# Decode attention over a 256 MiB cache: eight heads per unit, 8 MB loads into shared slots, P spread by masks, O picked on VectorE

## The chip, the cores and the metric

One core of a Trainium2 chip. The metric is the device time of one execution in microseconds (us). The core has TensorE (PE), VectorE (DVE), ScalarE (ACT), GpSimd (POOL), a SyncE queue (SP) that issues most loads, and sixteen DMA engines behind it. Ratios: the mean time of one kernel's fast runs over that of the kernel before in the same rounds, with a 95% interval, so not quite the ratio of the medians that are quoted beside them. Where I turn a ratio into us, I multiply by 670.5. The rounds of the experiments ran on three different chips (K15, K2, tail and all three edits on one, the three runs on rows and the one with two extra transposes on another, the rest on a third), so runs are compared through these ratios.

## The reference, cut to what matters

```python
xn = layernorm(x)                        # x: 4 x 1 x 640, bf16
q = (xn @ wq).reshape(B, Sq, H, Dh)      # B 4, H 32, Dh 128
scores = einsum('bhqd,bhkd->bhqk', q, k_cache) * Dh ** -0.5    # k_cache: 4 x 32 x 4096 x 128
p = softmax(scores)
o = einsum('bhqk,bhkd->bhqd', p, v_cache)
out = x + o.reshape(B, Sq, H * Dh) @ wo + gated_mlp(xn)
```

K and V are 134 MB each, every byte is used once, and there is one query per head. The weights add 14 MB.

## The kernel before

A unit is four heads of one batch entry: 4 MB of K or V, as 128 partitions with one row of 32 KB each. A group is the four units (batch entries) of the same heads. Units rotate through five whole tiles, and the tile framework inserts the waits.

```python
HG = 4; M = P // HG; T = Sk // M          # T = 128 tokens in a partition's row
kvpool = ctx.enter_context(tc.tile_pool(name="kvpool", bufs=5))      # 5 x 32 KB per partition

def load_unit(cache, key, u, cuts=(0, T)):
    g, b = divmod(u, B)
    t_sb = kv_tile(f"{key}{u}")
    src = cache[b, g * HG:(g + 1) * HG].rearrange("e (m t) d -> (e m) (t d)", t=T)
    for t0, t1 in zip(cuts[:-1], cuts[1:]):
        nc.sync.dma_start(out=t_sb[:, t0 * Dh:t1 * Dh], in_=src[:, t0 * Dh:t1 * Dh])

def emit_T(u, ch):                        # VectorE: 128x2048 f32 transpose in 32x32 blocks
    nc.vector.transpose(kT[:], kw[:, ch * n:(ch + 1) * n])
# ... (cut) emit_S: eight PE matmuls of 128x512 for each such block give the scores S in PSUM

def z_fill(g, bb):                        # ScalarE spreads the transposed P out of PSUM into Zb
    # ... (cut)
    nc.scalar.copy(out=dst, in_=src[:, 2 * bb + b1])

def emit_O(g, bb):                        # O of two units goes to SBUF, f32 matmuls select from it
    nc.scalar.copy(out=O_sb[:], in_=O_ps[:])

# the last V unit alone, token by token, so that O comes out with d on the partitions:
for t in range(T):
    nc.tensor.matmul(ol_ps[:], lhsT=vv[:, t, :], rhs=zc, start=(t == 0), stop=(t == T - 1))
nc.vector.tensor_tensor(out=oL[:, :, 3:4], in0=ol_ps[:, :, None], in1=..., op=ALU.mult)
emit_proj(g, oL, last=True)               # eight matmuls with wo
```

## Time and profile before

| | before |
|---|---|
| time | 670.65 us median of 3 (670.45 to 670.73) |
| span of the profiled execution | 668.2 us |
| bytes by DMA | 282.65 MB in 12,035 packets |
| DMA, busy | 98.7% of the span in one queue |
| DVE, PE, ACT busy | 48%, 50%, 9% |

How to read it: work on an engine that is half idle costs nothing unless something waits for it.

### The profile page before, as it was taken

To read this page: it belongs to the slowest core of one execution; us is meant where nothing else is said; L and a number is where in the kernel's file an instruction comes from. 1 tells how busy PE (TensorE), PEld (TensorE's weight loads), DVE (VectorE), ACT (ScalarE), POOL (GpSimd) and SP (SyncE) were. 2 spreads that over 40 slices of the span, in tenths; PEclk is the share of its full clock that TensorE was granted. 3 is DMA by queue.
4 is the path that set the end of the run, shared out by engine and by line. 5 is a ranking of instruction groups with operands and counts; after the bars stand their busy time and mean duration, and the time that the engine had idled before them with its cause. 6 is when DMAs were issued, how large, how long until landed. Compare 5 with 4: busy or idle time off the path is not lost.

```text
span 668.2 us, 6403 instructions
## 1 busy us (share of the span) xinstructions
PE 333.3 (50%) x2781; PEld 140.6 (21%) x2781; DVE 318.8 (48%) x252; ACT 60.4 (9%) x184; POOL 10.6 (2%) x43
## 2 busy tenths in 40 slices
PE   0646563456543654337455364345743365443645
PEld 0511121122111321113121031111311122111323
DVE  5179863365543455542555534346543345543300
ACT  1100210012000200003000030001200021000300
POOL 1100000000000000000000000000000000000000
PEclk9997577878777787666866677876777778567776
DMA  8999999999999999999999999999999999999996
GB/s 329 429 420 429 437 437 421 429 441 420 431 437 421 436 434 433 422 434 434 423 434 434 427 433 432 429 430 435 429 432 431 430 431 433 428 434 429 430 425 243
DMA packets 12035, 282.65 MB, mean 423 GB/s; under 512 B 1396, under 2 KB 2024, under 8 KB 3304
## 3 DMA queue, kind: packets, MB, share of 16 engines
q1 hardware_dynamic: 11928, 282.25, 98.7%
q8 instruction: 21, 0.34, 0.2%
q14 instruction: 6, 0.05, 0.0%
q0 software_dynamic: 64, 0.00, 0.0%
q10 hardware_dynamic: 16, 0.01, 0.0%
HBM read 282.25 MB, written 0.01 MB: 422 GB/s over the span
## 4 chain that ended last, share of the span: by engine, by line
DMA 66%; PE 12%; issue 11%; DVE 9%; ACT 2%; SPq 0%; DVEq 0%; ACTq 0%
DMA k<-in_A_k_cache_dram 52%; DMA v<-in_A_v_cache_dram 7%; DVE kT L323 6%; PE O L427 5%; DMA wo_last<-in_A_wo_dram 5%; PE S L341 3%; DMA wq<-in_A_wq_dram 2%; ACT p L369 2%; PE x L382 1%; PE misc L444 1%; PE misc L207 1%; DVE m L348 1%; PE misc L352 0%; DVE om L447 0%; ACT O_sb L435 0%
## 5 line engine op out<-in xcount | busy, mean ns | idle before, releaser
L323 DVE STREAM_TRANSPOSE kT<-k 128x2048 f32<-128x2048 f32 x128 | 284.6, 2280 | 216.7 <-DMA k<-in_A_k_cache_dram 214.3
L341 PE MATMUL S<-kT,QZ 128*32 128x512 bf16 x1024 | 200.8, 532 | 261.3 <-DVE kT L323 258.9
L341 PEld LDWEIGHTS <-QZ 128*32 128x32 bf16 x1024 | 57.0, 114 | 400.8 <-issue 390.0
L427 PE MATMUL O<-v,Zb 128*32 128x512 bf16 x992 | 91.1, 463 | 8.9 <-DMA v<-in_A_v_cache_dram 8.9
L427 PEld LDWEIGHTS <-Zb 128*32 128x32 bf16 x992 | 42.1, 111 | 38.8 <-issue 24.1
L369 ACT ACTIVATE p<-S,negmax 128x1024 bf16<-128x1024 f32 x16 | 17.7, 1110 | 271.9 <-DVE negmax L363 271.9
L435 ACT COPY O_sb<-O 128x512 f32<-128x512 f32 x16 | 9.4, 586 | 239.7 <-PE O L427 239.7
L393 ACT COPY Zb<-x 32x128 bf16<-32x128 bf16 x128 | 27.3, 254 | 10.2 <-PE x L382 9.5
L382 PE MATMUL x<-IdP,p 128*128 128x128 bf16 x128 | 16.1, 305 | 18.9 <-ACT p L369 18.6
L447 DVE SCALAR_TENSOR_TENSOR om<-misc,rinv,MkH 16x512 bf16<-16x512 f32 x7 | 5.2, 739 | 38.3 <-PE misc L444 38.3
L444 PE MATMUL misc<-O_sb,SelG 128*16 128x128 f32 x112 | 16.9, 289 | 2.0 <-DVE rinv L403 1.5
L382 PEld LDWEIGHTS <-p 128*128 128x128 bf16 x128 | 12.0, 138 | 22.7 <-ACT p L369 22.7
L280 POOL COPY QZ<-q 32x16 bf16<-32x16 bf16 x32 | 7.9, 248 | 443.7 <-PE S L341 430.6
L444 PEld LDWEIGHTS misc<-O_sb,SelG 128*16 128x16 f32 x112 | 10.2, 100 | 8.1 <-ACT O_sb L435 2.4
L479 DVE TENSOR_TENSOR oL<-misc,rinv 128x8 bf16<-128x8 f32 (+1 forms) x2 | 0.3, 168 | 22.6 <-PE misc L477 22.6
L348 DVE TENSOR_REDUCE m<-S 128x1 f32<-128x512 f32 x8 | 5.5, 692 | 10.9 <-PE S L341 10.9
L373 DVE TENSOR_TENSOR rowsum<-rs 128x1 f32<-128x1 f32 x8 | 1.2, 154 | 17.0 <-ACT p L369 17.0
L352 PE MATMUL misc<-dg,ones_f 128*128 128x128 f32 x16 | 4.2, 346 | 9.0 <-DVE dg L350 9.0
L207 PE MATMUL misc<-xnT,wq 128*128 128x4 bf16 x160 | 4.6, 166 | 7.7 <-DMA wq<-in_A_wq_dram 7.7
L207 PEld LDWEIGHTS <-wq 128*128 128x128 bf16 x160 | 4.4, 104 | 7.9 <-DMA wq<-in_A_wq_dram 7.9
L210 DVE CAST q_bf<-misc 128x128 bf16<-128x128 f32 x1 | 0.3, 292 | 12.0 <-PE misc L207 12.0
L465 PE MATMUL proj<-wo,oT 128*4 128x320 bf16 x56 | 5.0, 298 | 1.9 <-DVE oT L458 1.9
(95 smaller groups left out, 76.4 us busy)
## 6 DMA issues: line engine op xcount, KB each, us to landing
k<-in_A_k_cache_dram SPq DMA_DIRECT2D x32, 4096.0 KB, 43.0
v<-in_A_v_cache_dram SPq DMA_DIRECT2D x31, 4096.0 KB, 41.1
wo<-in_A_wo_dram SPq DMA_DIRECT2D x7, 640.0 KB, 45.8
wq<-in_A_wq_dram SPq DMA_DIRECT2D x1, 3072.0 KB, 12.2
w_gmlp<-in_B_w_in_dram SPq DMA_DIRECT2D x1, 2160.0 KB, 21.4
wq<-in_A_wq_dram SPq DMA_DIRECT2D x1, 2048.0 KB, 16.7
v<-in_A_v_cache_dram SPq DMA_DIRECT2D x1, 2048.0 KB
v<-in_A_v_cache_dram SPq DMA_DIRECT2D x1, 1024.0 KB, 38.4
```

The source lines that it names most:

```text
L207: nc.tensor.matmul(q_ps[:, h, :], lhsT=wq_t[c][:, h * Dh:(h + 1) * Dh], rhs=xnT[:, c, :], start=(c == 0), stop=(c == DC - 1))
L280: nc.gpsimd.tensor_copy(out=qz[r0:r0 + 32, :, :, 8 + 8 * hd], in_=q3[r0:r0 + 32, :, c0:c0 + B].rearrange("p a b -> p b a"))
L323: nc.vector.transpose(kT[:], kw[:, ch * n:(ch + 1) * n])
L341: nc.tensor.matmul(S_ps[32 * q:32 * q + 32, :, :], lhsT=qz[:, b, kw, w0:w0 + 32], rhs=kT[:, i, :, kw // 2, :, kw % 2], start=(b == 0 and c ...
L348: nc.vector.tensor_reduce(out=m1[:], in_=S_ps[:].rearrange("p k m -> p (k m)"), axis=AX.X, op=ALU.max)
L369: nc.scalar.activation(out=p_i[:], in_=S_ps[:, 8 * i:8 * i + 8, None, :].to_broadcast((P, 8, HG, M)), func=ACT.Exp, bias=negmax[:, 0:1], s ...
L382: nc.tensor.transpose(x[:, t, :], p_bf[t // 8][:, t % 8].rearrange("p h m -> p (h m)"), IdP[:])
L393: nc.scalar.copy(out=dst, in_=src[:, 2 * bb + b1])
L427: nc.tensor.matmul(O_ps[32 * q:32 * q + 32, :, :], lhsT=Zb[bb][:, w0:w0 + 32], rhs=vv[:, e // 16, e % 16, :, :], start=(b1 == 0 and e < 4) ...
L435: nc.scalar.copy(out=O_sb[:], in_=O_ps[:])
L444: nc.tensor.matmul(oh[:], lhsT=SelG[:, bb, c].rearrange("p h b -> p (h b)"), rhs=O_sb[:, c, :], start=(bb == 0 and c == 0), stop=(bb == 1 ...
L447: nc.vector.scalar_tensor_tensor(out=om[:], in0=oh[:, None, :].to_broadcast((G, HG, Dh)), scalar=state.pop(("rinv", g))[:, 0:1], in1=MkH[: ...
```

## The change

The intent: double the row and the load (64 KB and 8 MB), halve the number of groups (eight to four), and make wo's rows 10 KB. A unit no longer fits the old tile, so K, V and wo share one array of five 4 MB slots, placed by hand. The new shapes also change how P reaches the V matmuls and how O leaves them.

```diff
-    HG = 4
+    HG = 8
...
-    kvpool = ctx.enter_context(tc.tile_pool(name="kvpool", bufs=5))
+    SL = T * Dh // 2
+    kv = const.tile([P, 5 * SL], BF16)
...
+    place = {("k", 0): 3, ("k", 1): 0, ("k", 2): 2, ("k", 3): 0}
+    for u in range(B, NU):
+        place[("k", u)] = 1 if u % 2 == 0 else 0
+    for u in range(NU):
+        place[("v", u)] = 3
+    place[("v", NU - 3)] = 1
+    place[("v", NU - 1)] = 0
+    first = {2: 1}
+    cuts = {("k", 0): (0, T // 2, T), ("k", 1): (0, T // 2, T), ("v", NU - 1): (0, 128, 192, 224, 240, T)}
+    for g in range(NG):
+        u = B * g + B - 1
+        if u < NU - 1:
+            cuts[("k", u)] = (0, T // 2, T)
+            first[u] = 0
...  P: a dense copy xd of the transposed P, then one masked spread for each head
+                nc.vector.tensor_copy(out=xd[r0:r0 + 32, :, 16 * half:16 * half + 16],
+                                      in_=x[r0:r0 + 32, :, r0:r0 + 32].rearrange("p t r -> p r t"))
...
-                nc.scalar.copy(out=dst, in_=src[:, 2 * bb + b1])
+                    nc.scalar.activation(out=dst, in_=src, func=ACT.Copy, scale=MkE[r0:r0 + 32, e:e + 1])
...  O: four masked picks in place of a copy and f32 selections
-        nc.scalar.copy(out=O_sb[:], in_=O_ps[:])
+        nc.vector.tensor_scalar(out=R, in0=O_ps[:, 0, :], scalar1=Mk4[:, 0:1], scalar2=None, op0=ALU.mult)
+        for c in range(1, 4):
+            nc.vector.scalar_tensor_tensor(out=R, in0=O_ps[:, c, :], scalar=Mk4[:, c:c + 1], in1=R, op0=ALU.mult, op1=ALU.add)
...  the order of work: the next load is put out ahead of the work on the current one
+    for i, item in enumerate(seq):         # K0 K1 K2 K3 V0 K4 V1 K5 V2 ... K15 V12 V13 V14 V15
+        if i + 1 < len(seq):
+            load_unit(seq[i + 1])
...  wo: eight heads at once into slot 2, the last group's in pieces of 4, 2, 1 and 1 heads
-            for h0, h1 in ((0, 2), (2, 3), (3, 4)):
+            for h0, h1 in ((0, 4), (4, 6), (6, 7), (7, 8)):
```

The token-by-token treatment of the last V unit is dropped: V15 goes the common way, with picks and one selection.

## The prediction

> **What bounds the kernel now.** I read the page's first two parts, then the queue table and the list of issues, then busy time by stretches, then the chain at the end, and last the waits of the load queue.
>
> ```profile
> PE 333.3 (50%) x2781; PEld 140.6 (21%) x2781; DVE 318.8 (48%) x252; ACT 60.4 (9%) x184; POOL 10.6 (2%) x43
> ...
> DMA  8999999999999999999999999999999999999996
> ...
> DMA packets 12035, 282.65 MB, mean 423 GB/s; under 512 B 1396, under 2 KB 2024, under 8 KB 3304
> ...
> q1 hardware_dynamic: 11928, 282.25, 98.7%
> ```
>
> No compute engine passes 50%; the DMA engines are full in every slice but the first and the last, and one queue holds them 98.7% of the span. So only three things can move the time: bytes (unchanged), the pace at which full engines move them, and the stretches in which they are not full. The stretches show the last two:
>
> ```profile
> 0.00:20.00 20.00, 2.69 (x86) 2.53 (x87) 8.96 (x36) 2.86 (x3) 2.71 (x11) 1.00 0.85 345
> 40.00:80.00 40.00, 25.81 (x126) 6.97 (x121) 34.38 (x21) 0.51 (x1) 0.98 (x4) 0.73 1.01 432
> 160.00:320.00 160.00, 78.67 (x606) 31.31 (x602) 76.11 (x51) 13.60 (x44) 1.97 (x8) 0.74 1.00 430
> 480.00:600.00 120.00, 58.28 (x440) 21.96 (x440) 58.20 (x35) 7.38 (x23) 0.00 (x0) 0.73 1.00 431
> 660.00:668.20 8.20, 3.47 (x72) 2.42 (x72) 0.65 (x2) 0.00 (x0) 0.00 (x0) 0.50 0.24 87
> ```
>
> The last two numbers are the DMA share and GB/s. From 40 to 600 us the share is 1.00 at 430 to 432 GB/s. In the first 40 to 80 us DVE is busy 34.4 of 40 us, so there DVE is nearly as tight as DMA; later it is under half. At the end:
>
> ```profile
> 633.62 30.23 DMA wo_last<-in_A_wo_dram
> 663.85 0.04 issue
> 663.89 1.30 PE proj L465 x8
> ```
>
> After the last byte of wo only eight projection matmuls, a cast and the store remain, about 4.3 us to the span's end at 668.2. The queue's waits tell how far loads run ahead:
>
> ```profile
> SPq L294 <- DVE kT L323: 302.6, 32, 15.3
> ...
> k<-in_A_k_cache_dram SPq DMA_DIRECT2D x32, 4096.0 KB, 43.0
> v<-in_A_v_cache_dram SPq DMA_DIRECT2D x31, 4096.0 KB, 41.1
> ```
>
> The queue waits for buffers to come free most of the time, but a 4 MB load takes 9.7 us (4.19 MB at 432 GB/s) and lands 43 us after issue: more than three others are queued ahead of it. Waiting for a buffer costs nothing now.
>
> **What the Trainium skill says.** "DMA: Bandwidth & Descriptors", section "Where 436 GB/s comes from", puts the ceiling of a core's sixteen engines at 435.2 GB/s. The trace agrees: 430 to 432 over long stretches. The same page, "Why small descriptors are slow (HBM only)", gives a fixed cost per packet and per descriptor, so longer rows should help; at 32 KB rows little of it can be left, since 431 is already 99% of 435. "Perfetto Trace Analysis", section "Optimization Strategy", says that the same gap repeating on the engine that should be saturated can mean too little room for the next tile. Before has no such gap; after is the kernel in which to look for it. "VectorE: DVE Perf Modes", section "Why PSUM operands drop a tier", holds an f32 operand in PSUM to the 1x rate; the reduce of 128x512 f32 from PSUM at 692 ns agrees (1.35 ns an element with its fixed cost), so I cost the new DVE reads of PSUM at that.
>
> **Part by part.**
>
> *Loads.* K and V go from 64 loads of 4 MB with 32 KB rows to 32 units of 8 MB with 64 KB rows (some cut in halves); wo rows go from 5 to 10 KB. The first nine 4-us windows add to 13.71 MB by 36 us; the stretch after 650 us holds 4.64 MB. So 264.3 MB took 614 us, 430.4 GB/s. At 435.2 it would take 607.3 us: 6.7 us is all that rows and load count could ever return. I take half of it to hang on each load or packet, and halve that: **-1.7 us**. wo alone is under 2% of the bytes.
>
> *Buffers.* Five whole tiles of 4 MB become five slots of 4 MB, two to a unit, so one unit is being used, one loads, and half a unit is spare. Nearly all V units share slots 3 and 4; K alternates between slots 0-1 and 1-2 and frees slot 1 first. The load after next is therefore issued only when the current V is used up, or when half the current K is transposed. A bubble appears if that is later than the end of the transfer in flight. Two lags are needed. Landing: 8.55 MB of weights and 4.19 MB of K0 had been moved at 33.8 us (sum of windows), DVE started on it at 36.6: 2.7 us. Issue to first bytes: first issue 0.74 us, no byte before 1.5 us: about 1.2 us (estimate). An 8 MB load takes 19.4 us.
> Steady state: K needs 4 transposes x 2.28 = 9.1 us to free slot 1, while V loads for 19.4 us; slack 19.4 - 9.1 - 2.7 - 1.2 = 6.4 us. V needs 64 matmuls, 4 to 7.2 us at the 2.0 to 3.6 us per 32 that the timeline shows; slack at least 8 us. No bubble.
> First group: K0 lands in halves at 36.6 and 46.3, K1 at 55.9 and 65.6, K2 whole at 85.0, K3 at 94.7 and 104.4, V0 at 123.8. DVE is done with K1 at 74.6, idles to 85, then needs sixteen transposes in a row: 36 us, to 121. K4 needs K3's second half, so it is issued at 121.1 and flows at 122.3; V0's bytes ended at 121.1. **+1.2 us.** Then V1 waits until V0 is used: S done 122.9; maximum, broadcast and negation 3.6 (reduce of 1024 about 1.2); table load 1.3; seven of eight exponentials 4.8; two rounds of transposes, 32-partition copies (0.65 each) and mask spreads to about 139; last 32 matmuls to 142. K4's bytes end at 141.7. **About +1.5 us.**
> Later groups: K's halves land 9.7 us apart and 1.31 MB of wo (3.0 us) is queued before V, and exp's table is in place; slack about 8 us. The last group's K is not halved: V14 is issued some 37.4 us after K15 lands, V13's bytes end at 39.1. **+0.3 us** on average.
>
> *Engines.* The 1024 K transposes' matmuls, 128 DVE transposes of 128x2048 and 128 P transposes stay. DVE gains 64 picks of O (128x128 from PSUM, 0.29 each like the 128x128 mask multiply: 19 us) and 32 copies of the dense transpose (0.65: 21 us): 319 becomes about 360 us, 54%. ACT loses sixteen O copies (9.4) and gains about 24 us of mask spreads and 4 us of exponentials: about 79 us. PE loses most of the 112 f32 selection matmuls (17 us). None sets the end; all lie beside loads.
>
> *Tail.* wo_last doubles to 1.31 MB, all behind V15. V15 lands about 3 us earlier relative to wo's end; its last four matmuls, four picks (1.2), one selection (0.5) and a multiply fit in that. Fourteen of sixteen projection matmuls run before wo's last piece, against none of eight now. **-1.0 us.** The small x load leaves the tail (361 GB/s at 650 to 652 us): **-0.3 us.**
>
> Sum: -1.7 + 1.2 + 1.5 + 0.3 - 1.0 - 0.3 = 0.0.
>
> **Rivals.**
> 1. *Rows pay in full.* If the whole shortfall from 435.2 is per load or packet, long rows bring it near its ceiling: -5 to -7 us, some 664 us. For: the share is 1.00, so the loss is inside the engines' busy time. Against: instruction fetches and uneven engines would give the same share, and 32 KB rows are long.
> 2. *The shallow queue starves.* If landing lag or V's use is longer than I think, every load starts late. With 28 loads, 1 us each is 698 us, far slower. For: slack falls from about 30 us to 6-8. Against: the steady ledger holds no stall that DVE's 9.1 us or PE's 7 us could make.
> 3. *The softmax becomes the bound.* Longer groups delay the first V of each; if the two rounds take 8 us more than reckoned, four groups lose a few us each: about 680.
> 4. *Hidden anyway.* DMA is the bound in both, nothing changes beyond 1%.
>
> **Range and chances.** The fourth is likeliest; the first and a mild form of the third pull either way by 6 us. I predict 670.5 us, 664 to 677. Faster by 2% means under 657.5, which asks for 434 GB/s with no ramp lost: 0.03. Slower by 2% asks for 13 us of bubbles: 0.06. Same: 0.91.
>
> **What would show it.** Mid-run stretches at share 1.00 and 430 to 434 GB/s show the steady ledger right; a share under 0.97 there with the load queue waiting for PE or DVE shows rival 2. A dip near 121 and 142 us, and none at later group ends, shows the first-group step. The projection after the last wo wait should have two matmuls, not sixteen. DVE busy should be near 360 us. The prediction is wrong if 64 KB rows change the engines' own pace by more than 1%, or if reuse of slots waits on something other than the half I named.

## The result, and the profile after

| | before | after |
|---|---|---|
| time, same rounds | 670.55 us median of 4 (670.36 to 670.73) | 671.43 us median of 4 (670.96 to 671.51) |
| ratio | | 1.0012, 95% interval 0.9994 to 1.0029 |
| span of the profiled execution | 668.2 us | 669.6 us |

No change within the noise of the rounds. First the page's busy times, DMA row and queue line, then busy time by stretches (PE, PEld, DVE, ACT, POOL, granted clock, DMA share, GB/s), of the kernel after:

```profile
PE 304.9 (46%) x2575; PEld 126.4 (19%) x2575; DVE 357.5 (53%) x322; ACT 93.1 (14%) x232; POOL 7.6 (1%) x27
...
DMA  8999999999999999999999999999999999999995
...
DMA packets 8098, 282.64 MB, mean 422 GB/s; under 512 B 916, under 2 KB 2056, under 8 KB 2440
...
q1 hardware_dynamic: 7976, 282.24, 98.2%
```

```profile
160.00:320.00 160.00, 73.25 (x586) 29.29 (x587) 86.61 (x66) 21.80 (x56) 1.26 (x4) 0.71 1.00 432
320.00:480.00 160.00, 71.48 (x588) 29.05 (x585) 86.60 (x66) 21.80 (x56) 1.26 (x4) 0.72 1.00 433
480.00:600.00 120.00, 52.40 (x428) 19.49 (x423) 61.31 (x41) 3.61 (x8) 0.00 (x0) 0.70 1.00 433
600.00:640.00 40.00, 15.88 (x168) 8.44 (x168) 10.51 (x26) 21.80 (x56) 0.00 (x0) 0.71 0.97 410
```

The reader is to see three things. The packets fell by a third, so 64 KB rows do travel as longer packets. From 160 to 600 us the engines now move 432.6 GB/s on average against 430.6 before: 2 us gained in these 440 us. (The view counts a packet's whole time and bytes where it starts. So a share can pass 1, and a short stretch is coarse where packets of 64 KB take 2.4 us each; this is the "aliasing" of some expectations below.) And from 600 to 640 us, where before stood at full share, the share is 0.97. So something was gained mid-run and spent elsewhere. Two places where it could be spent are the first group and the tail. The load queue's issues in the first group (start, duration):

```profile
94.07 0.33 SPq L153 DMA_DIRECT2D kv<-in_A_v_cache_dram  x1
120.38 0.33 SPq L153 DMA_DIRECT2D kv<-in_A_k_cache_dram  x1
141.12 0.33 SPq L153 DMA_DIRECT2D kv<-in_A_v_cache_dram  x1
```

These are V0, K4 and V1. K4 is put out 0.7 us before the prediction's 121.1, V1 0.9 us before its 142. The tail, in order of time:

```profile
661.29 0.62 PE L455 MATMUL O<-kv,Zb 128*32 128x512 bf16 x4 [0.89 <-DMA kv<-in_A_v_cache_dram]
...
661.96 0.35 DVE L462 TENSOR_SCALAR R<-O,Mk 128x128 f32<-128x128 f32 x1 [11.68 <-PE O L455]
662.35 1.12 DVE L464 SCALAR_TENSOR_TENSOR R<-O,Mk,R 128x128 f32<-128x128 f32 x3
...
664.16 0.17 DVE L500 TENSOR_TENSOR oL<-misc,rinv 128x8 bf16<-128x8 f32 x1 [0.69 <-PE misc L499]
...
664.39 2.29 PE L492 MATMUL proj<-kv,oL 128*4 128x320 bf16 x16 [0.27 <-DVE oL L500]
```

The last piece of V15 is used at 661.29. Matmuls, four picks, the selection and the multiply take 3.0 us, and only then do sixteen projection matmuls begin, back to back: the projection waits for oL. The last piece of wo, with its time from issue to landing, and the projection of the kernel before, then the same piece of the changed kernel:

```profile
wo_last<-in_A_wo_dram SPq DMA_DIRECT2D x1, 160.0 KB, 11.7
663.89 1.28 PE L465 MATMUL proj<-wo_last,oL 128*4 128x320 bf16 x8 [0.27 <-DMA wo_last<-in_A_wo_dram]
```

```profile
kv<-in_A_wo_dram SPq DMA_DIRECT2D x1, 160.0 KB, 13.3
```

They were issued at 653.01 and 651.34 us, so wo's last piece landed at 664.7 in the kernel before and at 664.6 in the changed one: by then the two are level, and the 1.4 us between the spans lie behind it. The wait of 0.27 us before was for wo's first piece, not for its last; the row of eight was already running when the last landed.

### The profile page after: what moved, and what is told of

Read it like the earlier page. It is cut to its first block, busy times and chain, and to the rows that moved or that the text cites. A ratio compares the mean times of both kernels' runs of the same rounds, so it can differ in the third digit from the quotient of the medians.

```text
span 669.6 us, 6019 instructions
## 1 busy us (share of the span) xinstructions
PE 304.9 (46%) x2575; PEld 126.4 (19%) x2575; DVE 357.5 (53%) x322; ACT 93.1 (14%) x232; POOL 7.6 (1%) x27
## 3 DMA queue, kind: packets, MB, share of 16 engines
q1 hardware_dynamic: 7976, 282.24, 98.2%
## 4 chain that ended last, share of the span: by engine, by line
DMA 70%; DVE 14%; issue 12%; ACT 2%; PE 1%; SPq 0%; DVEq 0%; ACTq 0%
DMA kv<-in_A_k_cache_dram 65%; DVE kT L354 12%; DMA kv<-in_A_v_cache_dram 6%; ACT Zb L398 1%; DVE xd L420 1%; ACT p L412 1%; PE O L455 0%; PE proj L492 0%; PE x L416 0%; SPq L115 0%; DVE m L372 0%; PE S L365 0%; DVE R L464 0%; PE misc L377 0%; PE misc L499 0%
## 5 line engine op out<-in xcount | busy, mean ns | idle before, releaser
L354 DVE STREAM_TRANSPOSE kT<-kv 128x2048 f32<-128x2048 f32 x128 | 282.9, 2276 | 143.5 <-DMA kv<-in_A_k_cache_dram 143.5
L365 PE MATMUL S<-kT,QZ 128*32 128x512 bf16 x1024 | 187.9, 500 | 250.0 <-DVE kT L354 250.0
L455 PE MATMUL O<-kv,Zb 128*32 128x512 bf16 x1024 | 73.3, 440 | 26.2 <-DMA kv<-in_A_v_cache_dram 23.0
L398 ACT ACTIVATE Zb<-xd,MkE 32x256 bf16<-32x256 bf16 (+1 forms) x160 | 65.3, 454 | 95.6 <-PE O L455 87.1
L412 ACT ACTIVATE p<-S,negmax 128x512 bf16<-128x512 f32 x32 | 21.6, 693 | 319.8 <-DVE negmax L386 319.7
L462 DVE TENSOR_SCALAR R<-O,Mk 128x128 f32<-128x128 f32 x16 | 5.6, 351 | 101.6 <-PE O L455 101.6
L455 PEld LDWEIGHTS <-Zb 128*32 128x32 bf16 x1024 | 33.8, 108 | 64.0 <-issue 40.1
L420 DVE COPY xd<-x 32x512 bf16<-32x512 bf16 x32 | 22.0, 687 | 22.5 <-PE x L416 21.7
L464 DVE SCALAR_TENSOR_TENSOR R<-O,Mk,R 128x128 f32<-128x128 f32 x48 | 16.8, 351 | 1.7
L412 ACT ACTIVATION_READ_ACCUMULATOR p<-S,negmax 128x1 f32 x32 | 6.7, 210 | 0.0
```

Of the source, the lines that this page charges most:

```text
L354: nc.vector.transpose(kT[:].rearrange("p (t r) -> p t r", r=32), kw)
L365: nc.tensor.matmul(S_ps[32 * q:32 * q + 32, e], lhsT=QZ[:, b, 2 * kh + w, e, w0:w0 + 32], rhs=kb[:, i, :, e, :, w], start=(b == 0 and k < ...
L398: nc.scalar.activation(out=dst, in_=src, func=ACT.Copy, scale=MkE[r0:r0 + 32, e:e + 1])
L412: nc.scalar.activation(out=p_q[:, :, :, e, :], in_=S_ps[:, e, 8 * q:8 * q + 8, None, :].to_broadcast((P, 8, HP, M)), func=ACT.Exp, bias=ne ...
L420: nc.vector.tensor_copy(out=xd[r0:r0 + 32, :, 16 * half:16 * half + 16], in_=x[r0:r0 + 32, :, r0:r0 + 32].rearrange("p t r -> p r t"))
L455: nc.tensor.matmul(O_ps[32 * q:32 * q + 32, :, :], lhsT=Zb[b % 2][:, w].rearrange("p h c -> p (h c)"), rhs=vv[:, w * 4 * Dh:(w + 1) * 4 * ...
```

## The experiments

My theory, A: the kernel is bound by the DMA engines in both versions; longer rows make them about 2 us faster, and that is spent by loads put out too late in the first group, by a gap before V14, and by a longer tail. The rivals: B, the rows do not matter and the difference in pace is counting or chance; C, the gaps are hidden, because the engines are spread in time and the slowest never runs dry; D, eight-megabyte units in five slots leave no slack, and every small delay costs.

### Does the row length set the pace?

Three runs change only how long a contiguous piece is. The first splits every unit into two loads of 4 MB with 32 KB rows.

```diff
-        c = cuts.get(item, (0, T))
+        c = cuts.get(item, (0, T // 2, T))
```

> The changed kernel with every 8 MB unit loaded by two loads of 4 MB with 32 KB rows; slots, order and work as they are. From 160 to 600 us the kernel before moves 430.6 GB/s with 32 KB rows, the changed one 432.6 with 64 KB rows. Theory A (a fixed cost per row or load, so that longer rows pay): the pace falls back to 430.6, time 671.4 + 2.5 = 674. Rival B (the pace does not hang on rows; the difference of 0.5% is counting or the engines' skew): pace 432.6, time within 0.7 us of 671.4.

Measured: 673.17 us (672.55 to 674.17), ratio 1.0045 (1.0032 to 1.0057), against 1.0012 for the changed kernel: 2.2 us slower. Mid-run pace 431 GB/s in all three long stretches.

The other two keep 8 MB loads but take the pieces of a row from different units, so that they cannot be joined (results wrong on purpose, for 30 of the 32 units; the comparison with the reference did not flag it). Which units the pieces come from is clipped, so that with 4 KB pieces all whole units of a cache read the same 8 MB again; that this changes nothing by itself was not tested.

```diff
+                flat = bass.AP(flat.tensor, flat.offset, [[T * Dh, P], [P * T * Dh + n, a], [1, n]])
+                nc.sync.dma_start(out=dst[:, t0 * Dh:t1 * Dh].rearrange("p (a n) -> p a n", n=n), in_=flat)   # n = 8192 or 2048
```

> The changed kernel with the same 8 MB loads, but the source of each row taken from other units in pieces of 16 KB, so that one load moves four pieces per partition (results wrong on purpose; bytes, buffers and instructions the same). Theory A: the two paces above give 11 ns per row piece (1217.6 ns per 32 KB against 1211.9), so 16 KB pieces run at 427 GB/s and the time is about 680. Rival B (pace does not hang on rows): 671 to 672.

> As the run with 16 KB pieces, with pieces of 4 KB (results wrong on purpose). Theory A: 11 ns a piece, 162 ns per 4 KB, 404 GB/s, about 715 us. Rival B: 671 to 672. Rival C (the cost per piece is hidden until pieces are shorter than some size): 16 KB as 64 KB, 4 KB slower but by less than half of this.

Measured: 676.88 us with 16 KB pieces (ratio 1.0098, 1.0082 to 1.0113) and 701.99 us with 4 KB pieces (ratio 1.0474, 1.0459 to 1.0488). The packets and one mid-run stretch of the run with 4 KB pieces:

```profile
DMA packets 65058, 282.64 MB, mean 404 GB/s; under 512 B 916, under 2 KB 2056, under 8 KB 63880
```

```profile
160.00:320.00 160.00, 74.25 (x552) 28.31 (x550) 78.00 (x63) 21.80 (x56) 1.26 (x4) 0.68 1.02 410
```

The share stays at 1.02: the engines are as busy as ever and move less. The main queue carried 7,976 packets in the changed kernel, 11,720 with 4 MB loads, 18,856 with 16 KB and 64,936 with 4 KB pieces. Per engine (a sixteenth) that is 234, 680 and 3,560 more; the ratios give 2.2, 5.8 and 31 us more. Each packet more costs 9.4, 8.5 and 8.7 ns; with about 1.4 us of uncertainty in each difference, the first alone says little, the last is good to 5%. A size of load changed only in the first of the three, and the same cost explains all, so it hangs on the packet. The packet records of the traces say the same directly: the median packet of 64 KB took 2,420 ns, of 32 KB 1,215, of 16 KB 615 and of 4 KB 164, which is about 13 ns and then 27.2 bytes per ns (435 GB/s for sixteen engines). That the whole run pays some 9 and not 13 fits the share of 1.02: at 4 KB neighbouring packets of an engine overlap by about 4 ns (my estimate, 2.4% of 164). B falls. For the change itself: before has 11,928 packets in that queue, 247 more per engine than after, which at 8.6 ns is 2.1 us. That is the gain. The two paces, 2 us in two thirds of the run, would give nearly 3 for all of it.

### Are the late loads of the first group worth anything?

K2 is loaded in two halves and used first half first, so that VectorE need not wait for all of K2.

```diff
-    first = {2: 1}
-    cuts = {("k", 0): (0, T // 2, T), ("k", 1): (0, T // 2, T), ("v", NU - 1): ...
+    first = {2: 0}
+    cuts = {("k", 0): (0, T // 2, T), ("k", 1): (0, T // 2, T), ("k", 2): (0, T // 2, T), ("v", NU - 1): ...
```

> The changed kernel, with K2 loaded in two halves and used first half first, so that VectorE does not idle until K2 is whole and then run sixteen transposes in a row. Theory A (K4 and V1 are issued just too late in the first group, about 1.2 and 1.5 us): K4 is issued some 7 us earlier than at 120.4, V1 some 7 us earlier than at 141.1, the stretches at 122 to 124 and 140 to 142 us lose their dips (229 and 172 GB/s), time 671.4 - 2.5 = 668.9. Rival B (the dips are the aliasing of 64 KB packets, nothing is lost there): issues earlier, time within 0.5 us of 671.4.

Measured: 670.06 us (669.30 to 671.33), ratio 0.9994 (0.9982 to 1.0007): 1.2 us less than the changed kernel, about half of what was expected, and by itself within the two intervals. K4 was issued at 113.65 and V1 at 134.97, 6.7 and 6.2 us earlier. Two stretches of the changed kernel, then the same of this run:

```profile
100.00:120.00 20.00, 11.28 (x72) 3.79 (x72) 20.00 (x10) 0.00 (x0) 0.00 (x0) 0.91 1.02 440
120.00:146.00 26.00, 11.76 (x112) 6.86 (x112) 11.55 (x21) 19.29 (x49) 1.27 (x4) 0.73 0.99 407
```

```profile
100.00:120.00 20.00, 13.31 (x58) 3.88 (x53) 15.27 (x11) 1.07 (x1) 1.26 (x4) 0.59 1.02 440
120.00:146.00 26.00, 9.82 (x104) 6.29 (x106) 9.66 (x16) 18.34 (x49) 0.00 (x0) 0.63 1.01 437
```

In the first, VectorE is busy 20.00 of 20.00 us just before K4 can be put out, and the DMA rate falls to 407 afterwards; in the second both are gone. The gap was real: 26 us x (437 - 407) / 437 = 1.8 us of traffic. But this profiled execution was the slowest of the five, 671.33 us: in it the traffic was regained and the time was not. The table of landings below shows where it went.

### Is the gap before V14 worth anything?

The last group's K15 is halved like the others.

```diff
-        if u < NU - 1:
-            cuts[("k", u)] = (0, T // 2, T)
-            first[u] = 0
+        cuts[("k", u)] = (0, T // 2, T)
+        first[u] = 0
```

> The changed kernel, with the last group's last K unit loaded in two halves and used first half first, as the other groups have it. In the changed kernel V14 was issued 44.4 us after that K landed; the ledger had 37.4, and the DMA engines run at 229 and 131 GB/s in two stretches of 2 us near 617 and 621. Theory A (late release of V12's slots leaves the engines dry before V14, some 2.5 us): V14 is issued about 9 us earlier, no stretch near 617 to 622 is below the aliasing of 64 KB packets, time 671.4 - 2.5 = 668.9. Rival B (the dip is a hidden one, the engines catch up or the bound is elsewhere): V14 is issued earlier but the time stays within 0.5 us of 671.4.

One figure of that text is a misreading of mine. I took a load that the chain of waits shows from 623.97 us for V14. It is V15's last piece; the load queue put V14 out at 618.13, so 38.5 us after K15 landed at 579.6, not 44.4. The ledger's 37.4 was 1.1 us off, not 7.

Measured: 671.1 us (670.37 to 672.68), ratio 1.0013 (0.9999 to 1.0027): nothing gained. V14 was issued at 609.2, 9 us earlier, as expected. The stretches of the changed kernel and then of this run:

```profile
612.00:618.00 6.00, 6.00 (x65) 2.40 (x65) 2.55 (x5) 5.67 (x15) 0.00 (x0) 0.62 0.83 360
...
660.00:661.00 1.00, 0.40 (x4) 0.10 (x4) 0.00 (x0) 0.00 (x0) 0.00 (x0) 0.97 1.05 363
661.00:662.00 1.00, 0.62 (x4) 0.11 (x3) 0.04 (x1) 0.00 (x0) 0.00 (x0) 0.50 1.07 364
662.00:663.00 1.00, 0.00 (x0) 0.00 (x0) 0.93 (x3) 0.00 (x0) 0.00 (x0) 0.50 0.68 233
```

```profile
612.00:618.00 6.00, 0.00 (x0) 0.00 (x0) 0.00 (x0) 1.82 (x5) 0.00 (x0) 0.70 1.06 459
...
660.00:661.00 1.00, 0.37 (x8) 0.02 (x3) 0.00 (x0) 0.00 (x0) 0.00 (x0) 0.50 0.67 249
661.00:662.00 1.00, 0.60 (x4) 0.09 (x3) 0.35 (x1) 0.00 (x0) 0.00 (x0) 0.50 0.55 202
662.00:663.00 1.00, 0.00 (x0) 0.00 (x0) 0.89 (x3) 0.00 (x0) 0.00 (x0) 0.50 0.42 154
```

The gap at 612 to 618 us is closed (0.83 to 1.06). But look at the end. With the gap, the engines work until 662 us and stop nearly together. Without it, a third of their time is already idle at 660, and the last of them still work on until nearly 664. Each load leaves sixteen completion marks in the trace, which I take for one per engine, and they show this engine by engine. The marks of V13 lie 4.15 us apart in the changed kernel, those of V14, behind the gap, 2.0 us: its first came 2.7 us later than in this run, its last only 0.7 (641.55 against 640.86). wo's last piece landed at 664.66 and here at 664.22. So the traffic that the gap had delayed was for the most part that of engines that were ahead anyway, and C holds for most of this gap: while it is shorter than the engines' spread, it costs mainly the time of the fast ones. Why the slowest is slow no run here shows.

### Does the tail hang on V15's chain or on wo?

The last V unit alone is reduced token by token, as in the kernel before.

```diff
+        elif u == NU - 1:
+            for t in range(T):
+                nc.tensor.matmul(ol_ps[:], lhsT=vv[:, t * Dh:(t + 1) * Dh], rhs=Zb[b % 2][:, t // 4, :, t % 4],
+                                 start=(t == 0), stop=(t == T - 1))
+            nc.vector.tensor_tensor(out=state["oL"][:, :, b], in0=ol_ps[:], in1=state[("rinv", g)][:, :, b], op=ALU.mult)
```

> The changed kernel, with the last V unit alone reduced as the kernel before does it: 256 small matmuls that give O with d on the partitions, in place of 64 wide ones with four VectorE picks and a selection matmul. In the changed kernel 3.1 us pass from the landing of V15's last piece to oL, then all sixteen projection matmuls (2.3 us) run. Theory A (this chain, not the last bytes of wo, sets the end; the prediction's tail term had it hidden): oL 0.85 us after the landing, fourteen projection matmuls before wo's last piece, time 671.4 - 2.2 = 669.2. Rival B (wo's last piece sets the end anyway): time within 0.5 us of 671.4.

Measured: 670.54 us (670.08 to 671.15), ratio 1.0002 (0.9990 to 1.0015): 0.7 us less, a third of what was expected.

```profile
662.26 0.18 DVE L533 TENSOR_TENSOR oL<-ol,rinv 128x8 bf16<-128x8 f32 x1 [11.44 <-PE ol L531]
663.39 2.29 PE L492 MATMUL proj<-kv,oL 128*4 128x320 bf16 x16 [1.17 <-DMA kv<-in_A_wo_dram]
```

oL is ready at 662.44 instead of 664.33, as expected. But the projection then waits 1.17 us for wo's first piece, which landed at 663.35, and all sixteen matmuls run in one row from there. Pieces two to four landed at 664.14, 664.56 and 664.96, each shortly before its own matmuls, so no later wait shows, and by the last landing fourteen of the sixteen matmuls had started (a head's two every 0.27 us). In the changed kernel four of sixteen had started by then, and in the kernel before six of eight. So the overlap that was expected does take place once oL is early. What limits the gain is the first piece: in the changed kernel the chain through the picks bounds the end; take it away and wo's first piece bounds it 1 us earlier.

### All together, and in pairs

> All three edits together. Theory A (three separate losses on the path of a DMA-bound kernel, so they add): 671.4 - 2.5 - 2.5 - 2.2 = 664.2, faster than the kernel before by about 6 us (1%). Rival B (the engines' skew or a common limit sets the end): the sum is not reached, 668 or more. Rival C (one of the dips is already hidden): between 666 and 668.

Measured: 668.25 us (667.93 to 668.57), ratio 0.9967 (0.9955 to 0.9980). This is 3.0 us less than the changed kernel, clear of both intervals, and 0.3% less than the kernel before: the best version found. The sum of 7.2 us was not reached; the value falls just above the boundary given for rival B.

Two runs of pairs:

> K2 halved and the direct reduction of the last V unit, without the halved K15. Alone they gave about -1.2 and -0.7 us against the changed kernel (ratios to before 0.9994 and 1.0002 against 1.0012), the halved K15 alone nothing, all three together -3.0 us. Theory A (each edit is worth the same in any company): 671.4 - 1.9 = 669.5, so that the halved K15 is worth 1.1 us once the others are in. Rival B (the pair alone gives the whole): 668.3. Rival C (without the halved K15 the gap before V14 grows by what the others gain): 670 to 671.

> K2 and K15 halved, tail as in the changed kernel. Theory A (the engines' gaps at 122, 141 and 618 us are one loss, made up only when both ends are mended): about 671.4 - 2.3 = 669.1, with the direct tail worth the rest. Rival B (gaps are covered by the slowest engine's backlog; only K2 counts): 670.2, as K2 alone.

Measured: K2 with the tail 669.22 us (668.17 to 670.81), ratio 0.9981 (0.9969 to 0.9994), 2.1 us less; K2 with K15 669.72 us (669.39 to 670.36), ratio 0.9991 (0.9977 to 1.0004), 1.4 us less.

| edits in the changed kernel | us against it, from the ratios |
|---|---|
| K15 halved | +0.1 |
| K2 halved | -1.2 |
| direct tail | -0.7 |
| K2 and K15 | -1.4 |
| K2 and tail | -2.1 |
| all three | -3.0 |

K2 and the tail add. The halved K15 is worth nothing alone and about 0.9 us once the other two are in. With intervals of about 0.9 us either way on each ratio, and 1.2 on the changed kernel's own, only the last two rows stand clear.

The landings (the last of a load's sixteen marks) cut each profiled execution, one per kernel, into stretches. In us:

| edits | from K0's first half to V1 | V1 to V14 | V14 to wo's last piece | wo's last piece to the end |
|---|---|---|---|---|
| none | 128.0 | 477.5 | 23.1 | 5.0 |
| K15 halved | 128.3 | 476.6 | 23.4 | 5.1 |
| K2 halved | 126.3 | 478.4 | 23.3 | 5.0 |
| direct tail | 127.4 | 477.6 | 23.0 | 3.7 |
| K2 and K15 | 126.3 | 476.7 | 23.1 | 5.3 |
| K2 and tail | 126.0 | 477.2 | 23.1 | 3.9 |
| all three | 126.3 | 476.9 | 23.0 | 4.0 |

Each edit acts in a stretch of its own: K2 takes about 1.7 us from the first, the direct tail 1.2 to 1.3 us from the last, and the halved K15 0.5 to 0.9 us from the second against the changed kernel. In the execution with K2 alone V14 was issued at 618.29 us, no earlier than in the changed kernel (618.13), and half of what K2 had gained was lost again in the second stretch; with K15 halved too it was kept. How large the loss is in the executions without a profile stays open.

### How much slack do the slots leave?

Dead transposes ahead of the real ones in nine K units delay the freeing of slot 1 by a known time.

```diff
+                if k == 0 and u >= B and b != B - 1:
+                    for j in range(2):             # 4 in the second run
+                        idle = ktpool.tile([P, 2 * TC * 32], F32, tag="kT", name="kT")
+                        nc.vector.transpose(idle[:], unit(("k", u)).bitcast(F32)[:, 0:2 * TC * 32])
                 emit_K(u, k)
```

> The changed kernel with two dead VectorE transposes of 128x2048 (4.5 us) ahead of the real ones in nine K units (u of 4 to 14 that do not end a group). The prediction's steady slack between the freeing of slot 1 and the end of the V transfer was 6.4 us. Theory A (that ledger): the load of the next K is issued 4.5 us later, still in time; time within 1 us of 671.4. Rival B (the shallow queue is at its limit, small delays cost): 671.4 + 9 x 4.5 = up to 710.

> The changed kernel with four dead VectorE transposes (8.9 us) ahead of the real ones in the same nine K units, past the slack of 6.4 us that the prediction gave and that two of them (4.5 us, 672.0 us measured) did not use up. Theory A (the ledger of slots): each of the nine K loads is issued 2.5 us too late and each costs it: 671.4 + 9 x 2.5 = about 694, with the load queue waiting for VectorE and a DMA share under 0.97 from 160 to 600 us. Rival B (the two lags of 2.7 and 1.2 us are too large, or the spread of the engines hides gaps of 2 to 3 us): 671.4 to 680.

Measured: two extra transposes 672.0 us (ratio 1.0027, 1.0013 to 1.0041), 1.0 us slower over nine units that each lost 4.5 us of VectorE time. Four extra 687.97 us (ratio 1.0265, 1.0248 to 1.0282), 17 us slower. The stretches and the queue's waits (total, times, longest) of the latter:

```profile
160.00:320.00 160.00, 65.46 (x568) 27.82 (x566) 107.41 (x76) 21.80 (x56) 1.26 (x4) 0.72 0.98 420
...
480.00:600.00 120.00, 47.16 (x400) 18.43 (x401) 79.92 (x49) 3.61 (x8) 0.00 (x0) 0.71 0.96 407
```

```profile
SPq L153 <- DVE kT L354: 243.2, 17, 17.7
```

VectorE is busy only two thirds of these stretches, and yet it sets the pace: the share falls to 0.98 and 0.96, and the queue's wait for K's transposes grows to 243 us from 156. By the landings not all nine units cost: the loads behind u = 6 and 10 are K7 and K11, whose first half goes into slot 0, and they came in time. The seven others landed 2.0 to 3.7 us later after the load before than in the changed kernel. 17 us over seven is 2.4 us each; if each late load costs in full, the slack is 8.9 - 2.4 = 6.5 us, against 6.4 in the ledger. D falls for the kernel as it is: it has about the slack that was reckoned, and past it late loads cost.

## Why the prediction was right, point by point

The prediction was 670.5 us in a range of 664 to 677, with 0.91 for no change beyond 2%. Measured: 671.43 and no change. The fourth rival, that DMA is the bound in both, is what happened. The terms:

- **Loads, -1.7 us.** Right. The measured 8.6 ns a packet gives 2.1 us, and the mid-run paces 2 to 3 us. The guess that half of the shortfall from 435.2 GB/s hangs on rows was one I could not support then; at 8.6 ns in some 1,215 it was two thirds (0.7% of 1.1%), and 64 KB rows still pay half of that. Rival 1, rows paying 5 to 7 us, is out.
- **Steady state, no bubble.** Right: share 1.00, and a slack of about 6.5 against 6.4 us by experiment. Rival 2 is out.
- **First group, +1.2 and +1.5 us.** The step was right: both issues fell within 1 us of the times given and the cause was VectorE's row of sixteen transposes. The size was too large: with K2 halved V1 landed 1.7 us earlier, not 2.7, which agrees with the 1.8 us of missing traffic. The time returned by K2 alone was 1.2 us, for part of it was lost again before V14.
- **V14, +0.3 us.** Near: issue 38.5 us after K15's landing against 37.4, and a visible gap. Closing it brought V14's last landing 0.7 us forward; by the time of the run nothing was gained by closing it alone.
- **Tail, -1.0 us.** This step failed, in sign: from wo's last landing to the end it took 3.5 us before and 5.0 after. The text says that "Fourteen of sixteen projection matmuls run before wo's last piece, against none of eight now". Four of sixteen had started by then, and six of eight before. V15 did land 3.4 us ahead of wo's end, as reckoned, and the chain to oL took 3.0 us (the picks 1.5 with their gaps against 1.2), so it fitted. But every projection matmul needs oL, and fourteen of them take another 1.9 us, for which no time was left. "None of eight" was a misreading of the kernel before: the wait that ends at 663.85 is for wo's first piece, so there was less to gain. With the direct reduction the fourteen did run before the last piece, and that returned 0.7 us (1.3 in the profile).
- **x load, -0.3 us.** Not tested by itself.
- **Engines.** VectorE 357.5 us against "about 360"; right as a sum. The text says that the picks are costed at the reduce's rate from PSUM, but it took the 0.29 us of a multiply that reads SBUF; a pick from PSUM took 351 ns. ScalarE 93 us against "about 79": the spreads were mis-sized. A spread of 32x128 took 390 ns, where I had taken 254 from the copy of the kernel before, and one of 32x256 497 ns against 360. None of it is on the path mid-run.

As a balance: packets -2.1 us, first group and tail and K15 together +3.0 us (the best version gives them back), sum +0.9; measured +0.8 from the ratio. The balance closes within the intervals. The landings of single executions split the second term: about 1.7 us in the first group, 0.5 to 0.9 before V14, 1.2 to 1.3 in the tail.

That no change beyond 2% came out was not luck: no term is above 3 us, and 2% is 13. That the sum 0.0 came within 1 us was in part luck: the first group was put 1.0 us too high and the tail more than 2 us too low.

So the change moved the time little because its gain was small from the start, and late loads and a longer tail spent it: before, the engines ran at 430.6 of 435.2 GB/s, and 32 KB rows already paid only 8.6 ns in some 1,215 ns each.

## What to carry to other kernels

When the DMA engines are full, count packets: what longer rows can return is the number of packets saved per engine times the cost of one, here 8.6 ns, and that can be reckoned before anything is rewritten. A buffer scheme with bigger units has to be checked for slack, the time from the freeing of a slot to the end of the transfer in flight, at the start, at each group's end and at the last unit. At the end, count the matmuls that must still run after the last operand is ready, not only the chain that makes it. And a gap on sixteen engines that run apart can cost the run less than its size: here a gap of 1.0 us of traffic, with 4.15 us between the first and the last engine, held up the last by 0.7. So repair gaps together with whatever follows the last byte, and measure the whole.

## What the Trainium skill lacked or had wrong

- "DMA: Bandwidth & Descriptors", section "Why small descriptors are slow (HBM only)", names a fixed cost per packet and judges packetization only worth it at or below 256 B. It gives no time for rows of kilobytes. These runs show the cost for pieces of 4 to 64 KB: 8.5 to 9.4 ns a packet on its engine, 31 us in all at 4 KB. The 10.5 ns a packet of that page's section "Measured (HBM→SBUF, 128 partitions, SWDGE, issued from GpSimd)" is another quantity, the 0.67 us of a 4 KB transfer over its 64 packets, and cannot be set beside it.
- The same page warns that bulk loads go at the pace of the slowest engine, but gives no size. Here the sixteen completion marks of a load lay 2.0 to 4.8 us apart (4.8 for the last loads of the kernel before), and closing a gap of 1.0 us of mean traffic (6 us at share 0.83) moved the last landing by 0.4 us.
- "VectorE: DVE Perf Modes", section "The TRN2 errata — SBUF-src ops pay a fixed extra latency per instruction", puts a ScalarE operation from SBUF 52 cycles above one from PSUM (43 ns, an estimate at the 1.2 GHz of its table). The spread from SBUF with a mask as scale took 390 ns, 136 more than the copy of the same 32x128 from PSUM (254 ns). Layout and the scale changed too, and no run separates them.
- No page says how far several pieces of a last transfer land apart: the four of wo (640, 320, 160 and 160 KB) landed at 663.35, 664.14, 664.56 and 664.96 us with the direct tail, close enough for sixteen matmuls to run in one row (2.29 us) from the first.
